# Linear attention with a mixture of depths: one stretch of transposes, products and turns per slot, the first batch's numbers from its own 0/1 rows, and later relus

## The chip, the cores and the metric

The kernel runs on one core of one Trainium2 chip. The metric is the device time of one execution in microseconds (us); lower is better. The core has five engines with a queue of instructions each, which run in order and wait for one another by semaphores: TensorE (PE in the profile, its weight loads PEld), VectorE (DVE), ScalarE (ACT), GpSimd (POOL) and SyncE (SP), which here issues most of the transfers.

## The reference

Inputs are q, k, v (8 batches, 8 heads, 576 rows, 64 columns), a gate vector (512), two expert matrices w1 (512 x 1024) and w2 (1024 x 512), and a capacity of 128. All is f32.

```python
q_s = softmax(q, over the 64 columns)
k_s = softmax(k, over the 576 rows)
kv  = einsum('bhsd,bhse->bhde', k_s, v)
x   = einsum('bhsd,bhde->bhse', q_s, kv)   # heads side by side: x is (8, 576, 512)
scores = x @ w_gate                        # per batch
out = x
for each batch b:
    top = the 128 rows with the highest score
    ye  = relu(x[b, top] @ w1) @ w2
    out[b, top] = x[b, top] + sigmoid(scores[b, top])[:, None] * ye
```

So attention is computed for all rows, and the expert network for 128 of 576 rows of each batch.

## The kernel before

**Units and slots.** The work is cut into 16 units, four heads of one batch each, two to a batch. Slot s of the main program is built around unit s. For a unit the kernel takes the exponential of k (`k_exp`, ScalarE, L238) and copies v beside a column of ones (`v_copy`, L250, one buffer), multiplies k by v on TensorE (`kv_mm`, L262), and makes a weight of the result on VectorE (`kv_out`, L271 to L275). It takes the exponential of q (`q_exp`, L246), transposes it on TensorE (`q_t`, L299), copies it out of PSUM on ScalarE (L304), and multiplies (`x_mm`, L324): that is product x. VectorE takes row sums and scores from it (`x_sums`, L335 and L336, and `score`, L362), scales it (`x_scale`, L342, two halves), and SyncE stores it to the output (`x_store`, L353). Transposes and product x share two PSUM buffers: the next slot's transposes need this slot's scalings done.

**Choosing rows.** When a batch is complete (odd slots), `score_row` spreads its scores over all partitions by five transposes and two ScalarE copies (L379, L382). Five comparisons on VectorE give each row its rank (`compare`, L390), `hits` turns ranks into 0/1 rows (L406), and `find` multiplies them by a table of row numbers and scores (L415) and sums the result (L419 to L421). `fetch` reads the chosen rows back from the output by an indirect transfer from GpSimd's queue (L428, tile `xr`). `gate` and `gated` make the sigmoid (L450; L455, L456). `turn` transposes the fetched rows on TensorE (L463) and copies them on ScalarE (L469, tile `xT`). For the first batch the rows are chosen on the chip instead (`select`, L438 and L442: its own f32 0/1 rows in the buffer of `hT`), and the numbers come later, in slot 4, from a second `hits(0)` and `find(0)`.

**Expert work.** It is cut into pieces that a generator hands out; the due count of pieces rises by n at each `pieces(n)` of a slot. Batches 0 and 1 are computed alone (L488, L497; a piece counts two), the others in pairs by a scheme of seven block products instead of eight, with precombined weights and rows (L573, L624; a piece counts one). A pair has 56 units: seven steps of four pieces for the first matrix, then seven for the second. Units 0 to 63 are the two single batches, 64 to 119 pair 2 and 3, 120 to 175 pair 4 and 5, 176 to 231 pair 6 and 7. After a step come sums on VectorE (`add`, L584; `after_p3`, L584 and L599 to L601; `after_p4`, L604 and L605) or copies and relus on ScalarE (L581, L587). The steps of the second matrix end in output sums (`begin`, L632 and L633; `end`, L637). Two PSUM banks serve a pair, so a step that starts a bank anew must wait for the sum that reads it.

**Order.** `tc.manual_schedule()` holds the program's order on every engine: what is written first is queued first. A slot of 7 and later before the change runs on TensorE: transposes of q for unit s, k by v for unit s + 1, four units, product x, in even slots the find for the batch finished before, then units again, in odd slots a score row and a turn among them. Slots 3 to 6 are a loop of their own. After slot 15 the rest of the pairs follows, with the last batch's find at unit 160 and its turn at 174.

## Time and profile before

| what | us |
|---|---|
| median of three runs | 210.12 |
| lowest and highest | 209.05, 212.19 |
| profiled execution, its own time | 209.2 |
| its span, first to last instruction | 207.5 |
| TensorE busy | 187.3 |
| VectorE busy | 128.7 |
| ScalarE busy | 102.7 |
| GpSimd busy | 69.2 |

The transposes of q of slots 3 to 15 begin at 35.06, 44.01, 53.14, 62.39, 70.81, 82.40, 90.56, 99.20, 110.64, 121.40, 130.88, 141.28 and 151.84 us of the span; the last product ends at 199.4. TensorE's f32 products appear as two passes each, so a unit of the first matrix is four records and one of the second is two. A timeline row gives start, duration, engine, line, operation, output and inputs, shapes and the number of merged instructions; in brackets stands the idle time before it and what ended it. A group's row gives busy microseconds and the mean of one in ns. TensorE's records overlap by some 0.07 us at their ends, so starts are compared with starts.

### The profile page before, as it was taken

What the parts mean: (1) busy time and instruction counts of PE and PEld (TensorE: products, weight loads), DVE (VectorE), ACT (ScalarE), POOL (GpSimd) and SP (SyncE); (2) the same over time, 40 slices, a digit from 0 to 9 for tenths busy, and PEclk for the clock granted to TensorE, in tenths of its full rate; (3) what the DMA queues carried; (4) which work ended last, traced back from release to release, by engine and by line L of the source; (5) the groups of instructions that cost most, each with busy time, mean ns of one, the idle gap of its engine ahead of it and who ended that gap; (6) DMA issues with size and microseconds to landing.
All of it is one profiled execution on the core that took longest, in us unless ns stands there. A gap on an engine that the chain in (4) does not pass through costs nothing.

```text
span 207.5 us, 7034 instructions
## 1 busy us (share of the span) xinstructions
PE 187.3 (90%) x2925; PEld 158.9 (77%) x2927; DVE 128.7 (62%) x422; ACT 102.7 (49%) x168; POOL 69.2 (33%) x122
## 2 busy tenths in 40 slices
PE   6699799999999896999989999999899989999940
PEld 2477699976579883769879888799899879998830
DVE  7236985498189345965993998269949934535010
ACT  2453344866668738946496495728243222322100
POOL 8022200200870742089824133135012264601230
PEclk9889999999999999999999999999999999999995
DMA  5999999999989899958977868959136113110020
GB/s 171 349 374 386 372 369 386 362 346 335 284 282 294 236 336 360 343 158 267 353 268 221 297 173 275 259 165 263 57 86 155 40 51 104 51 52 5 3 101 13
DMA packets 35210, 46.68 MB, mean 225 GB/s; under 512 B 2401, under 2 KB 28001, under 8 KB 35170
## 3 DMA queue, kind: packets, MB, share of 16 engines
q1 hardware_dynamic: 33616, 41.62, 62.2%
q0 software_dynamic: 1280, 4.20, 6.1%
q8 instruction: 25, 0.41, 0.8%
q10 hardware_dynamic: 274, 0.33, 0.5%
q14 instruction: 15, 0.12, 0.2%
HBM read 34.61 MB, written 11.53 MB: 222 GB/s over the span
## 4 chain that ended last, share of the span: by engine, by line
PE 49%; DVE 16%; DMA 12%; ACT 7%; POOL 5%; issue 5%; SPq 1%; POOLq 0%; ACTq 0%; DVEq 0%
PE mm L624 15%; PE mm L573 11%; DMA v<-in_v_dram 8%; PE x L324 7%; DVE junk L390 6%; PE tp L262 4%; PE mm L488 4%; DMA k<-in_k_dram 2%; PE mm L442 2%; PE x L299 2%; DMA q<-in_q_dram 2%; POOL tw L540 2%; ACT ke L238 2%; DVE xs L342 1%; SPq L121 1%
## 5 line engine op out<-in xcount | busy, mean ns | idle before, releaser
L390 DVE SCALAR_TENSOR_TENSOR junk<-srow,s,stairs 128x576 bf16<-128x576 f32 x40 | 35.2, 880 | 5.2 <-ACT srow L382 3.0
L324 PEld LDWEIGHTS x<-kv_w,qT 64*64 64x64 f32 (+1 forms) x1120 | 21.8, 135 | 7.5 <-ACT qT L304 3.8
L304 ACT COPY qT<-x 128x640 f32<-128x640 f32 (+1 forms) x30 | 17.8, 643 | 18.5 <-PE x L299 10.5
L324 PE MATMUL x<-kv_w,qT 64*64 64x66 f32 (+1 forms) x1120 | 24.6, 224 | 1.9 <-ACT qT L304 1.4
L262 PE MATMUL tp<-v_ones,ke 128*64 128x65 f32 x640 | 23.4, 230 | 2.3 <-DVE v_ones L250 1.7
L342 DVE TENSOR_TENSOR xs<-x,qrec 128x640 f32<-128x640 f32 x32 | 24.7, 815 | 0.0
L262 PEld LDWEIGHTS tp<-v_ones,ke 128*64 128x64 f32 x640 | 21.1, 143 | 4.0 <-issue 2.3
L624 PE MATMUL mm<-w,hT 128*128 128x256 f32 x96 | 22.9, 383 | 0.2 <-ACT hT L604 0.2
L428 POOL DMA_INDIRECT xr<-out_dram,idx x8 | 8.1, 1016 | 44.0 <-DVE no L421 16.1
L246 ACT ACTIVATE qe<-q 128x640 f32<-128x640 f32 (+1 forms) x32 | 20.2, 687 | 2.6 <-DMA q<-in_q_dram 2.6
L238 ACT ACTIVATE ke<-k 128x1280 f32<-128x1280 f32 x16 | 20.4, 1276 | 0.9 <-DMA k<-in_k_dram 0.9
L624 PEld LDWEIGHTS mm<-w,hT 128*128 128x128 f32 x96 | 17.6, 190 | 2.8 <-ACT hT L604 0.5
L335 DVE RECIPROCAL qrec<-x 128x10 f32<-128x10 f32 x32 | 7.0, 218 | 19.1 <-PE x L324 18.9
L573 PE MATMUL mm<-xT,w 128*128 128x128 f32 x144 | 18.4, 278 | 0.0
L624 PE MATMUL mm<-tw,hT 128*128 128x256 f32 x72 | 17.4, 382 | 0.7 <-DVE o L637 0.7
L573 PEld LDWEIGHTS mm<-xT,w 128*128 128x128 f32 x144 | 17.1, 192 | 0.5
L250 ACT COPY v_ones<-v 128x1280 f32<-128x1280 f32 x12 | 15.1, 1260 | 4.3 <-DMA v<-in_v_dram 4.3
L488 PE MATMUL mm<-xT,w 128*128 128x128 f32 x128 | 16.8, 282 | 0.0
L497 PE MATMUL mm<-w,hT 128*128 128x512 f32 x32 | 16.2, 614 | 0.0
L488 PEld LDWEIGHTS mm<-xT,w 128*128 128x128 f32 x128 | 15.0, 191 | 0.6
L624 PEld LDWEIGHTS mm<-tw,hT 128*128 128x128 f32 x72 | 13.4, 190 | 2.5 <-DVE o L637 0.8
L364 POOL TENSOR_TENSOR s<-s_all,valid_r 128x5 f32<-128x5 f32 x8 | 1.6, 198 | 40.6 <-DVE s_all L362 40.5
(138 smaller groups left out, 302.0 us busy)
## 6 DMA issues: line engine op xcount, KB each, us to landing
q<-in_q_dram SPq DMA_DIRECT2D x32, 288.0 KB, 6.4
v<-in_v_dram SPq DMA_DIRECT2D x16, 320.0 KB, 5.8
out_dram<-xs SPq DMA_DIRECT2D x16, 320.0 KB, 4.8
k<-in_k_dram SPq DMA_DIRECT2D x15, 320.0 KB
k<-in_k_dram SPq DMA_DIRECT2D x16, 256.0 KB
v<-in_v_dram SPq DMA_DIRECT2D x16, 256.0 KB, 5.3
out_dram<-xs SPq DMA_DIRECT2D x16, 256.0 KB, 5.1
w<-in_moe_w_dram SPq DMA_DIRECT2D x4, 512.0 KB
```

Source lines behind the costliest of these rows:

```text
L238: nc.scalar.activation(out=ke, in_=raw["k"][u % LD], func=AF.Exp)
L246: nc.scalar.activation(out=st["qe", u][:, r0:r1], in_=qr[:, r0:r1], func=AF.Exp)
L250: copy(out=v_ones[:, :, :, :D], in_=raw["v"][u % LD])
L262: nc.tensor.matmul(out=kv[part(h), i], lhsT=ke[:, 2 * h + i, r], rhs=vo[:, 2 * h + i, r], start=(r == 0), stop=(r == N2))
L304: nc.scalar.copy(out=to, in_=src)
L324: nc.tensor.matmul(out=to[:, r * C:(r + 1) * C], lhsT=lhsT, rhs=kw[part(i), a], start=True, stop=True)
L342: nc.vector.tensor_mul(xs[b][:, :, qd, :, a].rearrange("p r i d -> p i r d"), x[:, :, :, :D], rec.to_broadcast([P, 2, R, D]))
L390: nc.vector.scalar_tensor_tensor(junk, st["srow", b], st["s", b][:, r:r + 1], not_before[r], op0=OP.subtract, op1=OP.is_ge, accum_out=st[" ...
L488: nc.tensor.matmul(out=h_ps[:, f % HT * m:(f % HT + 1) * m], lhsT=w1[:, d, f * P:(f + 1) * P], rhs=xT[:, d, :m], start=(d == 0), stop=(d = ...
L497: nc.tensor.matmul(out=st["y", b][:m], lhsT=st["hT", b][:, f // HT, f % HT, :m], rhs=w2[:, f], start=(f == 0), stop=(f == KF - 1))
L573: nc.tensor.matmul(out=out_ps[:, f * m:(f + 1) * m], lhsT=w[:, k, f * P:(f + 1) * P], rhs=x()[:, k], start=first and f == 0 and k == 0, st ...
L624: nc.tensor.matmul(out=ps_of[to][:m, :HD], lhsT=st["hT", a][:, n, f, :m], rhs=w[:, f], start=first and f == 0, stop=f == HT - 1, skip_grou ...
```

## The change

It has three parts.

- **First batch's numbers.** `find_selected(0)` is called right after the products of slot 2. It copies the table of numbers to f32 on GpSimd and multiplies the f32 0/1 rows that `select` made by it; the three small sums (`found`) follow after `kv_out(3)`. The `hits(0)` and `find(0)` of slot 4 go; batch 1 takes their place there, one step earlier. `gate(0)` moves to slot 3, `gated(0)` to slot 4.
- **Relus.** The two relus of a pair that follow a sum (after steps 2 and 5) are issued after the second piece of the next step instead of right after the sum.
- **Slots 7 to 15.** The four units between k by v and product x go. In odd slots the turn stands between k by v and product x; so transposes, k by v, turn and product x are one stretch, with three units ahead of product x in slot 15 alone. The copy of v for slot s + 2 follows product x (in slot 7 it follows the score row and the exponential of k). The two scalings stand apart, with three units between them in odd slots and two in even ones. The other units follow the score row or the find. In slot 6 the exponential of k for slot 8 moves ahead of the gate.

```diff
+    def find_selected(b):
+        wide = md.tile([P, R, NV], F32, tag="wide", name="wide", bufs=1)
+        nc.gpsimd.tensor_copy(out=wide, in_=vals[:, place(b)])
+        hit = st["select"][1]
+        c_ps = bank("tp", 2)
+        for r in range(R):
+            nc.tensor.matmul(out=c_ps[:m, :NV], lhsT=hit[:, r, :m], rhs=wide[:, r], start=(r == 0), stop=(r == N2))
+        return lambda: found(b, c_ps)
...
         def after_p2():
             add("side1", 0)
-            relu(0)
         def after_p7():
             add("chain1", 3)
-            relu(3)
...
+        later = {id(after_p2): lambda: relu(0), id(after_p7): lambda: relu(3)}
...
+                    then = [lag] if lag and f == 1 else []
+                    if f == HT - 1:
+                        then.append(after)
...
     x_mm(2, 1)
+    found_0 = find_selected(0)
...
     kv_out(3)
+    found_0()
...
-            hits(0 if first else here)
-        if s == FIRST + 2:
+            hits(here)
+        if first:
             gated(0)
...
-            find(0 if first else here)
-            if first:
-                hits(here)
-            else:
-                fetch(here)
+            find(here)
+            fetch(here)
...
-            pieces(3)
-            gate(0 if first else here)
-            if first:
-                find(1)
-                fetch(1)
-                gate(1)
+            pieces(2)
+            if s == SETTLED - 1:
+                k_exp(s + 2)
+            pieces(1)
+            gate(here)
             prepared(PREPARE[s])
             if s == SETTLED - 1:
-                k_exp(s + 2)
                 v_copy(s + 2, nc.scalar)
...
         if on:
             kv_mm(s + 1)
             q_exps(s + 1)
+        if odd:
+            turn(ends - 1)
+        if on:
             kv_out(s + 1)
-            if s + 2 < NU:
-                v_copy(s + 2, nc.scalar)
-        if odd:
-            gated(ends - 1)
-        pieces(4 if on else 3)
+        else:
+            pieces(3)
         attend(s)
         if not odd:
             find(here)
             fetch(here)
-        scale(s)
+        if more and s > SETTLED:
+            v_copy(s + 2, nc.scalar)
+        x_scale(s, 0)
+        if odd:
+            gated(ends - 1)
+        pieces(3 if odd else 2)
+        x_scale(s, 1)
+        x_store(s)
         if s + 3 < NU:
             load(s + 3, "q")
...
-        if s + 2 < NU and not odd:
-            k_exp(s + 2)
-        pieces(2 if s < PAIRED or not on else 4)
         if odd:
+            if not on:
+                pieces(1)
             score_row(here)
-            if s + 2 < NU:
+            if more:
                 k_exp(s + 2)
-        left = 4 if s < PAIRED - 1 else 3 if s < PAIRED else 5
-        if odd and on:
-            compares(here, 1)
-            pieces(left // 2)
-            turn(ends - 1)
+                if s == SETTLED:
+                    v_copy(s + 2, nc.scalar)
             if ends > 2:
                 size(ends - 1)
             if ends > 2 and ends % 2 == 0:
                 combine_rows(ends - 2, ends - 1)
-            compares(here, 1)
-            pieces(1)
-            compares(here, 1)
-            pieces(left - left // 2 - 1)
...
+            if on:
+                compares(here, 1)
+                pieces(3 if many else 2)
+                compares(here, 1)
+                pieces(4 if many else 2)
+                compares(here, 1)
+                pieces(3 if many else 2 if s == PAIRED - 1 else 3)
+            else:
+                compares(here, 3)
+                pieces(4)
+                compares(here, 2)
+                hits(here)
+                pieces(2)
+        else:
             pieces(2)
...
+            if more:
+                k_exp(s + 2)
+            pieces(2)
             gate(here)
             prepared(PREPARE.get(s, 0))
-            pieces(left - 1)
+            pieces(7 if many else 4)
```

`many` holds from slot 10 on, `more` while a slot s + 2 exists, `on` while a slot s + 1 exists. A slot hands out 10 units in slots 7 and 8, 9 in slot 9 and 13 in slots 10 to 14, as before; slot 15 hands out 13 instead of 11.

More of the change, by code (lines that the diff above doesn't have):

```diff
@@ L416, in find, with found @@
                              start=(r == 0), stop=(r == N2))
+        found(b, c_ps)
+    def find_selected(b):
[6 more added lines that the diff above has]
+        return lambda: found(b, c_ps)
+    def found(b, c_ps):
         no = sl.tile([P, 2], F32, tag="no", name="no", bufs=4)
@@ L648, in pair, with piece @@
                   ("chain2", 3, tw2[:, 2], False, lambda: end("chain2", b, 0, rows=st["xr", b], last=True))]
+        def piece(product, what, f, then):
+            product(*what, f)
+            for step in then:
+                step()
+        lag = None
         for steps, product in ((steps1, product1), (steps2, product2)):
@@ L651, in pair @@
                 for f in range(HT):
-                    yield 1, lambda what=what, f=f, product=product, after=after: (
-                        product(*what, f), after() if f == HT - 1 else None)
+                    then = [lag] if lag and f == 1 else []
+                    if f == HT - 1:
+                        then.append(after)
+                    yield 1, lambda product=product, what=what, f=f, then=then: piece(product, what, f, then)
+                lag = later.get(id(after))
     def single(b):
@@ L918 @@
         kv_out(s + 1)
+        if s == FIRST:
+            gate(0)
         if odd:
@@ L940 @@
         here = ends if odd else ends - 1
-        on = s + 1 < NU
+        on, more = s + 1 < NU, s + 2 < NU
+        many = s >= PAIRED
         q_t(s, 0)
@@ L982 @@
                 combine_rows(ends - 2, ends - 1)
-            compares(here, 1)
-            pieces(1)
-            compares(here, 1)
-            pieces(left - left // 2 - 1)
-        elif odd:
-            compares(here, 3)
-            pieces(4)
-            compares(here, 2)
-            hits(here)
+            if on:
[12 more added lines that the diff above has]
+        else:
             pieces(2)
-            turn(ends - 1)
-            size(ends - 1)
-        else:
-            pieces(1)
+            if more:
+                k_exp(s + 2)
+            pieces(2)
             gate(here)
             prepared(PREPARE.get(s, 0))
-            pieces(left - 1)
+            pieces(7 if many else 4)
     last = B - 1
```

## The prediction

> **What bounds the kernel now.** I read the page first: busy shares and granted clock.
>
> ```profile
> PE 187.3 (90%) x2925; PEld 158.9 (77%) x2927; DVE 128.7 (62%) x422; ACT 102.7 (49%) x168; POOL 69.2 (33%) x122
> PEclk9889999999999999999999999999999999999995
> ```
>
> TensorE is busy for 90% of the span, and from the fourth slice to the last but one its granted clock is 0.9 or more. So time is won only where TensorE waits or does less. Next I read who TensorE waited for (columns: microseconds in total, times, longest):
>
> ```profile
> PE x L324 <- ACT qT L304: 1.4, 2, 1.2
> PE tp L463 <- ACT srow L382: 1.6, 1, 1.6
> PE tp L415 <- DVE hit L406: 1.1, 2, 0.7
> PE mm L624 <- DVE o L637: 0.7, 1, 0.7
> ```
>
> With a 0.60 in slot 7 (below) these are nearly all of its waits from slot 3 on: 1.1 for the 0/1 rows in slots 4 and 14 (L415), 1.6 for the turn of slot 7, 1.4 for copies of turned q in slot 10, 0.7 for an output sum in the last stage. Some 5.4 us can be won, no more. The cause of the copies' wait is on ScalarE: its relu stands first in its queue and waits for VectorE's sum.
>
> ```profile
> ACT hT L587 <- DVE hT L584: 13.9, 6, 3.9
> ```
>
> Then TensorE in order of time, for slots 9 to 11 and the last stage (columns: start, microseconds, line, shapes, count):
>
> ```profile
> 94.11 0.73 PE L324 MATMUL x<-kv_w,qT 64*64 64x66 f32 x33
> 95.44 1.16 PE L573 MATMUL mm<-xT,w 128*128 128x128 f32 x8
> 96.44 0.71 PE L379 MATMUL tp<-ident,s_all 128*128 128x128 f32 x5
> 96.98 0.61 PE L573 MATMUL mm<-xT,w 128*128 128x128 f32 x4
> 97.72 0.66 PE L463 MATMUL tp<-ident,xr 128*128 128x128 f32 x4
> 98.22 1.06 PE L573 MATMUL mm<-xT,w 128*128 128x128 f32 x8
> 99.20 0.78 PE L299 MATMUL x<-ident,qe 64*128 64x64 f32 x18
> 99.91 1.39 PE L262 MATMUL tp<-v_ones,ke 128*64 128x65 f32 x40
> 101.23 2.05 PE L573 MATMUL mm<-xc,sw 128*128 128x128 f32 x16
> ...
> 106.30 0.28 PE L415 MATMUL tp<-vals,hit 128*128 128x5 bf16 x5
> ...
> 166.91 1.99 PE L624 MATMUL mm<-tw,hT 128*128 128x256 f32 x8 [0.72 <-DVE o L637]
> ...
> 174.36 3.73 PE L573 MATMUL mm<-xT,w 128*128 128x128 f32 x32
> 177.93 3.74 PE L573 MATMUL mm<-xc,sw 128*128 128x128 f32 x32
> ```
>
> From start to start these give the prices that I use: transposes of q 0.70 (99.20 to 99.91), k by v 1.32 (to 101.23), product x 1.33 (94.11 to 95.44), score row 0.54 (96.44 to 96.98), a turn 0.50 (97.72 to 98.22). Eight units of expert work (32 records) take 3.57 (174.36 to 177.93), so one unit is 0.44. From 166.91, where unit 160 begins, TensorE hardly stops to the end, so what the change does to the start of unit 160 it does to the time.
>
> **The change part by part, up to the end of product x in slot 9.** Before, that is 95.44, with 68 units done.
>
> ```profile
> 28.14 2.94 PE L442 MATMUL mm<-hT,xs 128*128 128x128 f32 x24
> ...
> 51.11 0.28 PE L415 MATMUL tp<-vals,hit 128*128 128x5 bf16 x5 [0.46 <-DVE hit L406]
> 51.25 1.96 PE L497 MATMUL mm<-w,hT 128*128 128x512 f32 x4
> ...
> 72.19 1.39 PE L262 MATMUL tp<-v_ones,ke 128*64 128x65 f32 x40 [0.60 <-ACT v_ones L250]
> ```
>
> *First batch's numbers.* Five products in f32 are added after slot 2, each as two passes. No row has a pass with 128 columns of weights and five of data. The nearest in weights is L442, 24 passes in 2.94, 0.12 each, so 1.2 at most; the bf16 form took 0.14 for five (51.11 to 51.25), so 0.3 for ten at least. The weights are those of L442, so I take 1.1. TensorE runs without a wait there: it is on the path. Removed in slot 4 is the second find with its wait, 0.46 + 0.14 = 0.60. The copy of numbers on GpSimd, the three small sums and the missing 0/1 rows on VectorE lie beside TensorE's work there.
>
> *Slot 7.* The copy of v for slot 9 moves behind the score row and the exponential of k, so the turn's wait of 1.60 goes. The turn itself now stands behind k by v, at 72.19 + 1.32 = 73.51, and needs the rows fetched in slot 6:
>
> ```profile
> 68.95 1.00 POOL L428 DMA_INDIRECT xr<-out_dram,idx  x1 [7.71 <-DVE krec L271]
> ```
>
> ```profile
> DMA to landing us min/median/max: 3.4/4.3/5.2
> ```
>
> Landing 3.4 to 5.2 after 68.95 is 72.35 to 74.15: a wait of 0 to 0.65; I take 0.3. Product x, and all behind it on TensorE, is queued behind that turn. The 0.60 before k by v stays, because the exponential and the copy of v that it waits for still come behind the relu.
>
> *Slot 8.* ScalarE, the copy of v done, still has a size and a relu ahead of the copies of turned q:
>
> ```profile
> 78.65 1.26 ACT L250 COPY v_ones<-v 128x1280 f32<-128x1280 f32 x1 [4.29 <-DMA v<-in_v_dram]
> ...
> 83.30 1.16 ACT L304 COPY qT<-x 128x640 f32<-128x640 f32 x2
> ```
>
> The copy can't start before 78.65, when v has landed, whatever TensorE does. With product x drawn forward over four units, the two copies (1.16) are late by something between nothing and their own length; with TensorE some 1.3 ahead there I take 0.3. In exchange TensorE goes from k by v to x without expert work between them, two changes of operand shape fewer: eight passes before the transposes of q took 0.98 (98.22 to 99.20) against 0.89 by the unit's price, so 0.1 a change, -0.2.
>
> *Order.* By the end of product x in slot 9 four units fewer are done (-1.76) and one turn more (+0.5). Sum: 1.1 - 0.6 - 1.6 + 0.3 + 0.3 - 0.2 - 1.8 + 0.5 = -2.0, that is 93.4 with 64 units done.
>
> **From there VectorE decides.** In every even slot the find stands directly behind product x and waits for the 0/1 rows, and they come behind five comparisons. VectorE's prices:
>
> ```profile
> 93.51 0.15 DVE L455 TENSOR_SCALAR g<-g 128x1 f32<-128x1 f32 x1
> ...
> 99.63 0.42 DVE L548 TENSOR_TENSOR xc<-xT 128x256 f32<-128x256 f32 x1
> ...
> 155.53 0.22 DVE L335 RECIPROCAL qrec<-x 128x10 f32<-128x10 f32 x1 [0.16 <-PE x L324]
> ...
> 156.12 1.54 DVE L342 TENSOR_TENSOR xs<-x,qrec 128x640 f32<-128x640 f32 x2
> ...
> 160.32 0.69 DVE L584 TENSOR_TENSOR hT<-mm,hT 128x512 f32<-128x512 f32 x1
> ...
> 162.98 0.81 DVE L390 SCALAR_TENSOR_TENSOR junk<-srow,s,stairs 128x576 bf16<-128x576 f32 x1
> ...
> 165.03 0.82 DVE L406 TENSOR_TENSOR hit<-slot_no,rank 128x640 bf16<-128x640 f32 x1
> 165.78 0.68 DVE L605 TENSOR_TENSOR hT<-hT 128x512 f32<-128x512 f32 x1
> 166.38 0.48 DVE L637 SCALAR_TENSOR_TENSOR o<-mm,g,o 128x256 f32<-128x256 f32 x1
> ```
>
> ```profile
> L390 DVE SCALAR_TENSOR_TENSOR junk<-srow,s,stairs 128x576 bf16<-128x576 f32 x40 | 35.2, 880 | 5.2 <-ACT srow L382 3.0 <-POOL s L365 1.2
> ```
>
> Sums to the first scaling 0.6 (155.53 to 156.12), two scalings 1.54, the gate's pair 0.3, a pair of combined rows 0.85, a comparison 0.88, one sum 0.69, the four of after_p3 2.66 (160.32 to 162.98), hits 0.82, the subtraction of after_p4 0.68, an output sum 0.48.
>
> Slot 9 to find in 10: VectorE 0.6 + 1.54 + 0.3 + 0.85 + 4.4 + 0.69 + 0.82 = 9.2; TensorE eight units 3.5, score row 0.54, q 0.7, k by v 1.32, x 1.33, changes of shape 0.3: 7.7. So it waits 1.5, and the find is at 102.6. Before, four units were done by 106.30; this wait takes the place of the 1.2, which the later relu does remove. Then find, 13 units, q, k by v, turn, x: 0.14 + 5.7 + 0.7 + 1.32 + 0.5 + 1.33 + 0.2 = 9.9: slot 11's x ends at 112.5.
>
> Slot 11 to 12: VectorE 0.6 + 1.54 + 0.3 + 2.66 + 4.4 + 0.68 + 0.82 = 11.0, TensorE 13 units and the rest 9.9: a wait of 1.1, find at 123.5. Unit 104 needs an output sum that is now queued on VectorE behind kv_out, the sums to the first scaling and that scaling: in time, or late by up to about 0.9 with six units (2.6) as cover. I add 0.45. Slot 13's x: 123.5 + 9.9 + 0.45 = 133.9.
>
> Slot 13 to 14: VectorE 0.6 + 1.54 + 0.3 + 0.85 + 3 x 0.48 + 4.4 + 0.82 = 9.95 against 9.9: nothing. Find 143.8. Unit 132 needs the sum of unit 127, which stands behind the second scaling: 0 to 1, I add 0.5. With q, turn and three units in front of x, slot 15's x ends 9.9 + 0.5 later, at 154.2.
>
> Slot 15: VectorE 0.6 + 1.54 + 0.3 + 2.66 + 4.4 + 0.68 + 0.82 + 0.48 = 11.5, TensorE 20 units 8.8 and 0.7: it waits 2, and unit 160 starts at 165.7 against 166.91. I round the gain to 1.0, since hand-overs between engines are left out.
>
> The profiled execution took 209.2 (span 207.5, 1.7 around it), 0.9 under the median of 210.12 and close to the fastest run. The sum is 208.2 on the profile and 209.1 on the median; I take 208.7.
>
> **Moved at no cost.** A slot's store and its load of q go to SyncE's queue some three units later, behind the second scaling; the q that waits there is used two slots on, some 18 us, and would cost only if it came that late. The fetch stands in GpSimd's queue ahead of the weights' sums as before; from slot 8 on its find lies ten or thirteen units, q and k by v ahead of the turn, 6.4 or 7.7, against 5.2 for the longest landing and about 1 for the sums between find and fetch. The copy of v behind product x has the units after it as cover, 1.26 against 4.4 or more; if they were gone, k by v of the next slot would wait for all of it.
>
> **Rivals.** *TensorE stays the bound.* If comparisons come soon enough, none of the new waits appears: 1.6 + 1.4 + 0.7 + 0.7 + 0.6 go, four changes of shape (0.8) too, 1.1 is added: -4.7, 204.5 on the profile. For it: in slot 10 of before the find waited for nothing (the row at 106.30 shows no idle time). Against: five comparisons alone are 4.4 and no part of the change takes work from VectorE after slot 4.
>
> *GpSimd stretches comparisons (slower).* Comparisons differ widely:
>
> ```profile
> L390 DVE SCALAR_TENSOR_TENSOR junk<-srow,s,stairs x40: 799/819/2189, 23.1 to 163.8; 128x576 bf16<-128x576 f32 x40
> ```
>
> ```profile
> L633 POOL TENSOR_TENSOR o<-o,xr x9: 714/725/1314, 122.3 to 194.8; 128x256 f32<-128x256 f32 x9
> ```
>
> The longest is 2189 ns against a median of 819, and a sum on GpSimd took 1314 instead of 725 while comparisons ran at 163. If each stretch between x and find has such meetings (two with the combined rows in slots 9 and 13, one each in 11 and 15), six at 0.72 add 4.3 to stretches that VectorE now sets: 212.5 on the profile. It decides from the second meeting on, which eats the 1.0. Against: my 0.88 is a mean that holds some of them already. [...]
>
> *The change doesn't free ScalarE.* The relu two pieces on may still find its sum undone, since the sum stands behind comparisons; copies then wait as before and the time is 209 to 210.
>
> **How the numbers follow.** Forecast 0.58 (207 to 210), TensorE stays the bound 0.15 (204.5 to 206), stretched comparisons 0.19 (210.5 to 213), ScalarE not freed 0.08. The range reaches to the middle of the first and third: 205.4 to 211.8. About 2% is what a measurement of this kernel can tell from no change, 4.2 us: faster by more than that 0.14, within 0.81, slower by more 0.05.
>
> **What would show it.** Right: TensorE's waits at L463 for the srow copy and at L324 for qT gone; new waits of 1 to 2 us at L415 for hit in slots 10 and 12 and in the last stage; f32 find near 1.1. Wrong: if no wait at L415 exceeds 0.5 in slots 10 to 15, VectorE isn't the bound and the time falls to 205; if TensorE waits at L463 for the DMA by over 1 us in several slots, the fetch is too late, and the time rises.

## The result, and the profile after

The changed kernel takes 211.0 us (median of 20 executions, 208.39 to 212.67) against 209.37 for the kernel before (20 executions, 206.74 to 212.81). The ratio is 1.010 with a 95% interval of 1.0062 to 1.0138: slower by about 1%, where 208.7 was forecast, a gain. Ratios here and below leave out an execution that lies more than 1.5% above its kernel's fastest, so the medians of all executions stand beside them.

The profiled execution after took 210.88 us (span 209.1) against 209.2 (207.5). Line numbers have moved: `fetch` is L441, the turn L476, its copy L482, the pair's products L586 and L636, the sums L597, `end` L649; `find` (L415), `hits` (L406) and `compare` (L390) are where they were. First the page's shares and clock, and TensorE's waits from slot 7 on, beside the 0.60 in slot 7 that stays:

```profile
PE 189.0 (90%) x2930; PEld 160.6 (77%) x2932; DVE 127.5 (61%) x421; ACT 102.8 (49%) x168; POOL 70.2 (34%) x123
PEclk9999999999999999999999999999999969999996
```

```profile
PE tp L415 <- DVE hit L406: 5.0, 3, 2.0
PE tp L476 <- DMA xr<-out_dram,idx: 0.8, 1, 0.8
PE tp L476 <- DVE krec L271: 0.3, 1, 0.3
PE mm L586 <- DVE o L649: 0.2, 1, 0.2
```

The waits for the srow copy (1.6), for qT (1.2 in slot 10) and for the last output sum (0.7) are gone, and so is the second find of slot 4 with its 0.46. In their place stand three waits for 0/1 rows, 5.0 together, and two short ones in front of the turns. One digit of the clock line is new, too: a 6 in the 33rd slice, just behind the last find. TensorE in order of time:

```profile
30.72 1.28 PE L426 MATMUL tp<-wide,hT 128*128 128x5 f32 x10
31.93 1.39 PE L262 MATMUL tp<-v_ones,ke 128*64 128x65 f32 x40
...
73.24 0.63 PE L476 MATMUL tp<-ident,xr 128*128 128x128 f32 x4 [0.33 <-DVE krec L271]
...
91.47 0.63 PE L476 MATMUL tp<-ident,xr 128*128 128x128 f32 x4 [0.84 <-DMA xr<-out_dram,idx]
...
93.35 0.38 PE L586 MATMUL mm<-xT,w 128*128 128x128 f32 x1
...
102.61 0.28 PE L415 MATMUL tp<-vals,hit 128*128 128x5 bf16 x5 [1.52 <-DVE hit L406]
...
124.01 0.28 PE L415 MATMUL tp<-vals,hit 128*128 128x5 bf16 x5 [1.47 <-DVE hit L406]
...
142.99 0.50 PE L262 MATMUL tp<-v_ones,ke 128*64 128x65 f32 x9 [0.17 <-issue]
143.43 1.08 PE L324 MATMUL x<-kv_w,qT 64*64 64x66 f32 x32
...
145.17 0.28 PE L415 MATMUL tp<-vals,hit 128*128 128x5 bf16 x5
...
155.24 0.94 PE L586 MATMUL mm<-xT,sw 128*128 128x128 f32 x6
...
166.86 0.28 PE L415 MATMUL tp<-vals,hit 128*128 128x5 bf16 x5 [2.05 <-DVE hit L406]
167.25 3.11 PE L636 MATMUL mm<-tw,hT 128*128 128x256 f32 x8
170.16 4.23 PE L636 MATMUL mm<-w,hT 128*128 128x256 f32 x16
174.22 1.03 PE L636 MATMUL mm<-tw,hT 128*128 128x256 f32 x4
175.09 0.60 PE L476 MATMUL tp<-ident,xr 128*128 128x128 f32 x4
```

Up to the find in slot 10 this is the forecast to the tenth; the find in slot 12 comes 0.5 later than forecast. The new thing is at 167.25: eight products that took 1.99 before take 3.11, and the turn follows 8.2 us behind the last find. The view of windows shows why; its boundaries are put on a grid of 3.413 us on which all changes of the granted clock in these traces fall; here it falls at 167.98, rises at 171.39 and falls again at 205.52, 34.13 or ten times 3.413 later (columns: window, length, busy time and count of PE, PEld, DVE, ACT, POOL, granted clock, DMA share, GB/s):

```profile
161.15:164.56 3.41, 3.41 (x17) 2.88 (x16) 3.34 (x8) 0.47 (x1) 0.72 (x1) 1.00 0.11 37
164.56:167.98 3.42, 1.26 (x10) 0.87 (x9) 3.05 (x10) 0.68 (x2) 0.90 (x2) 1.00 0.00 0
167.98:171.39 3.41, 3.41 (x9) 2.66 (x9) 0.20 (x2) 0.47 (x1) 1.26 (x2) 0.50 0.28 77
171.39:174.80 3.41, 3.41 (x17) 3.00 (x16) 0.86 (x2) 0.00 (x0) 1.25 (x2) 1.00 0.31 82
```

In the window that holds the wait TensorE is busy for 1.26 of 3.42 us. In the next one it works without a pause, at half the clock, and gets through 9 records instead of 17. That is 1.7 us lost behind a wait of 2.05.

VectorE and GpSimd show why the wait is 2.05 (VectorE's rows and GpSimd's, each in order of time):

```profile
155.96 0.81 DVE L342 TENSOR_TENSOR xs<-x,qrec 128x640 f32<-128x640 f32 x1
...
162.12 1.17 DVE L390 SCALAR_TENSOR_TENSOR junk<-srow,s,stairs 128x576 bf16<-128x576 f32 x1
...
165.54 1.27 DVE L406 TENSOR_TENSOR hit<-slot_no,rank 128x640 bf16<-128x640 f32 x1
```

```profile
161.95 0.72 POOL L645 TENSOR_TENSOR o<-o,xr 128x256 f32<-128x256 f32 x1 [4.13 <-ACT o L644]
165.40 0.72 POOL L645 TENSOR_TENSOR o<-o,xr 128x256 f32<-128x256 f32 x1 [2.72 <-ACT o L644]
```

One comparison (1.17 instead of 0.82) and the 0/1 rows themselves (1.27 instead of 0.82) run beside a sum on GpSimd and take 0.8 longer together. These are meetings of the second rival, 0.35 and 0.45 each where it took 0.72, and they come in the stretch on VectorE that TensorE then waits for.

### The profile page after: what moved, and what is told of

The parts are those of the page before. It is cut to its first block, busy times and chain, and to the rows that moved or that the text cites. A ratio compares the mean times of both kernels' runs of the same rounds, so it can differ in the third digit from the quotient of the medians.

```text
span 209.1 us, 7044 instructions
## 1 busy us (share of the span) xinstructions
PE 189.0 (90%) x2930; PEld 160.6 (77%) x2932; DVE 127.5 (61%) x421; ACT 102.8 (49%) x168; POOL 70.2 (34%) x123
## 4 chain that ended last, share of the span: by engine, by line
PE 65%; DVE 20%; DMA 5%; issue 4%; ACT 1%; POOL 1%; POOLq 0%; DVEq 0%; ACTq 0%
PE mm L586 13%; PE mm L636 13%; PE x L324 10%; PE tp L262 7%; PE mm L501 7%; DVE junk L390 7%; PE mm L510 5%; DVE xs L342 4%; PE x L299 3%; DMA xr<-out_dram,idx 3%; DMA v<-in_v_dram 2%; PE mm L455 2%; PE tp L476 2%; PE x L292 1%; DVE o L649 1%
## 5 line engine op out<-in xcount | busy, mean ns | idle before, releaser
L390 DVE SCALAR_TENSOR_TENSOR junk<-srow,s,stairs 128x576 bf16<-128x576 f32 x40 | 33.7, 843 | 1.1 <-ACT srow L382 0.2
L324 PE MATMUL x<-kv_w,qT 64*64 64x66 f32 (+1 forms) x1120 | 25.2, 224 | 0.6 <-DVE qT L302 0.4
L342 DVE TENSOR_TENSOR xs<-x,qrec 128x640 f32<-128x640 f32 x32 | 25.2, 814 | 0.0
L262 PE MATMUL tp<-v_ones,ke 128*64 128x65 f32 x640 | 22.5, 224 | 1.2 <-ACT v_ones L250 0.6
L636 PE MATMUL mm<-w,hT 128*128 128x256 f32 x96 | 23.0, 389 | 0.0
L262 PEld LDWEIGHTS tp<-v_ones,ke 128*64 128x64 f32 x640 | 20.1, 137 | 3.0 <-issue 1.3
L441 POOL DMA_INDIRECT xr<-out_dram,idx x8 | 8.1, 1016 | 39.9 <-DVE krec L271 18.2
L636 PEld LDWEIGHTS mm<-w,hT 128*128 128x128 f32 x96 | 18.4, 196 | 2.5
L636 PE MATMUL mm<-tw,hT 128*128 128x256 f32 x72 | 18.3, 401 | 0.1
L586 PE MATMUL mm<-xT,w 128*128 128x128 f32 x144 | 17.8, 277 | 0.2 <-DVE o L649 0.2
L586 PEld LDWEIGHTS mm<-xT,w 128*128 128x128 f32 x144 | 16.9, 192 | 0.7 <-DVE o L649 0.6
L636 PEld LDWEIGHTS mm<-tw,hT 128*128 128x128 f32 x72 | 14.0, 198 | 2.5 <-DVE o L649 0.6
L645 POOL TENSOR_TENSOR o<-o,xr 128x256 f32<-128x256 f32 x9 | 6.9, 772 | 26.7 <-ACT o L644 26.1
L510 PE MATMUL mm<-w,hT 128*128 128x512 f32 x32 | 15.3, 605 | 0.0
```

The source lines that it names most:

```text
L262: nc.tensor.matmul(out=kv[part(h), i], lhsT=ke[:, 2 * h + i, r], rhs=vo[:, 2 * h + i, r], start=(r == 0), stop=(r == N2))
L324: nc.tensor.matmul(out=to[:, r * C:(r + 1) * C], lhsT=lhsT, rhs=kw[part(i), a], start=True, stop=True)
L342: nc.vector.tensor_mul(xs[b][:, :, qd, :, a].rearrange("p r i d -> p i r d"), x[:, :, :, :D], rec.to_broadcast([P, 2, R, D]))
L390: nc.vector.scalar_tensor_tensor(junk, st["srow", b], st["s", b][:, r:r + 1], not_before[r], op0=OP.subtract, op1=OP.is_ge, accum_out=st[" ...
L510: nc.tensor.matmul(out=st["y", b][:m], lhsT=st["hT", b][:, f // HT, f % HT, :m], rhs=w2[:, f], start=(f == 0), stop=(f == KF - 1))
L586: nc.tensor.matmul(out=out_ps[:, f * m:(f + 1) * m], lhsT=w[:, k, f * P:(f + 1) * P], rhs=x()[:, k], start=first and f == 0 and k == 0, st ...
```

## The experiments

The theory after the result: the new waits for 0/1 rows take up what slots 7 to 9 win, and the last one, 2.05 long, lets the clock fall for one window, which makes the loss. Rivals: the wait itself, without the clock, is the price; the first part's f32 products are the price; the later relus are.

**e1_busy.** TensorE is kept at work during the last wait, by products whose result nothing reads.

```diff
+    junk_x = ps.tile([P, 2, 512], F32, tag="x", name="x", bufs=2)
+    for _ in range(9):
+        nc.tensor.matmul(out=junk_x[:, 0], lhsT=ones_b[:, :P], rhs=ones_b, start=True, stop=True)
     find(last)
```

> The changed kernel with nine products of ones (bf16, 512 columns, into an unused PSUM tile) put ahead of the last find, where TensorE waited 2.05 us; nothing reads them. Theory (the long wait at the last find makes TensorE's granted clock fall to half for one window of 3.4 us): the nine take some 1.9 us in the place of the wait, unit 160 starts at 167 to 167.6 as in the changed kernel, the granted clock stays 1.00 from 165 to 175 us, and the time falls by 1.7 to about 209.3, a ratio to the kernel before of 1.00. [...]

Measured: 209.77 (207.54 to 211.07), ratio 1.0035 (0.9986 to 1.0084) to a median of 210.05 before. TensorE:

```profile
165.41 2.11 PE L1034 MATMUL x<-ones_b 128*128 128x512 bf16 x9
167.62 0.28 PE L415 MATMUL tp<-vals,hit 128*128 128x5 bf16 x5
...
174.16 0.60 PE L476 MATMUL tp<-ident,xr 128*128 128x128 f32 x4
```

From find to turn it is 6.5 us instead of 8.2, with the same real work and the find no earlier behind its comparisons, and the granted clock is 1.00 from 165 to 173. Useless work in the wait takes the fall of the clock away, and by the medians 1.2 us with it (two measurements on different chips, with intervals that overlap). The clock is part of the price.

**e2_find_late.** Find and fetch of slots 10, 12 and 14 stand behind four units instead of directly behind product x.

```diff
-        if not odd:
+        if not odd and not many:
             find(here)
             fetch(here)
...
             pieces(2)
+            if many:
+                find(here)
+                fetch(here)
```

> The changed kernel with find and fetch of slots 10, 12 and 14 put behind four units instead of directly behind product x. Theory (these finds wait for VectorE's comparisons, 1.5 us each in slots 10 and 12): both waits at L415 go, product x of slot 15 ends some 3 us earlier than in the changed kernel (152.3 against 155.2), and the time falls by 2.5 to 3, to about 208.3, a ratio of 0.995, with the wait at the last find still there. Rival (the fetched rows come too late for the turn in the next slot, now four units nearer): the turns of slots 11 and 13 wait 1 to 2 us each and the time stays near 211, a ratio of 1.01.

Measured: 221.11 (219.82 to 224.42), ratio 1.0596 (1.0523 to 1.0669). The waits at the finds of slots 10 and 12 are gone, but the turns wait for their rows instead, and three windows fall to half clock (behind waits of 3.08, 3.75 and 2.0):

```profile
PE tp L476 <- DMA xr<-out_dram,idx: 9.2, 5, 3.7
PE tp L415 <- DVE hit L406: 2.0, 1, 2.0
```

The edit did two things: it put the fetch late, and behind the slot's store, which touches the same tensor as the fetch reads. In slot 10 the landing took from 105.54 to 111.78, 6.2 us; in slot 14 the fetch wasn't issued until the store just ahead of it had ended. So it shows what a late fetch costs (more than the rival expected), and not what a late find would.

**e3_before_wait.** The kernel before, with the last batch's last comparison done four times (the same numbers each time), so that its last find waits.

```diff
             compares(here, 2)
+            for _ in range(3):
+                compare(here, R - 1)
             hits(here)
```

> The kernel before with the last comparison of the last batch done four times instead of once (the same numbers are written), so that the 0/1 rows come 2.6 us later. Theory (a wait of over 2 us at the last find makes the clock fall): TensorE waits 2.5 us there, the granted clock falls to half for 3.4 us right behind it, and the time grows by 2.6 + 1.7 = 4.3, a ratio of 1.02. Rival (no fall by a wait of this length): it grows by 2.6, a ratio of 1.0125, and the clock stays 1.00.

Measured: 213.73 (211.68 to 215.54), ratio 1.0221 (1.0154 to 1.0288).

```profile
170.12 0.29 PE L415 MATMUL tp<-vals,hit 128*128 128x5 bf16 x5 [2.91 <-DVE hit L406]
```

```profile
171.00:173.00 2.00, 1.88 (x5) 1.52 (x6) 0.67 (x6) 0.20 (x1) 1.01 (x1) 0.50 0.00 0
173.00:175.00 2.00, 2.00 (x6) 1.64 (x5) 0.00 (x0) 0.06 (x1) 0.00 (x0) 0.50 0.44 131
```

A wait of 2.91 is put into a kernel that had none there, and the clock is halved from 170.15 to 176.98, two windows. The loss, 3.7 us by the medians, is more than the wait.

**e4_tail.** The changed kernel, with eight more units between the third and the fourth comparison of the last batch, so that its find stands behind unit 168 instead of 160, and the turn six units later.

```diff
-                pieces(4)
+                pieces(12)
                 compares(here, 2)
                 hits(here)
-                pieces(2)
...
-    upto(last_pair - 16)
+    upto(last_pair - 8)
     find(last)
...
-    upto(last_pair - 12)
+    upto(last_pair - 4)
...
-    upto(last_pair - 2)
+    upto(last_pair + 4)
     turn(last)
```

> The changed kernel with the last stage in another order: twelve units instead of four between the third and the fourth comparison of the last batch, its find at unit 168 instead of 160 and its turn at 180 instead of 174. Theory (the wait at the last find and the clock that falls behind it cost 2.0 + 1.7): no wait over 0.3 at the last find, granted clock 1.00 to the end, time lower by 3 to 3.7, about 207.5, a ratio of 0.99. Rival (the time is moved to the last turn, whose rows come late, or to VectorE's later sums): TensorE waits over 1.5 us at the last turn or behind it and the time stays at 210 to 211, a ratio of 1.005 to 1.01.

Measured: 207.94 (207.06 to 210.85), ratio 0.9957 (0.991 to 1.0004) to 210.05. The find at 167.61 waits for nothing, the clock is full from 5.5 to 200.09, and TensorE's last product starts at 197.69 instead of 201.06. Product x of slot 15 ended 0.48 earlier by itself, so 2.9 us are won by moving the last find: 2.05 of wait and 1.7 of clock, less a new wait of 0.79 for a sum at 178.27.

**e5_find_three and e6_both.** e5: find and fetch of slots 10, 12 and 14 behind three units, but ahead of the scalings and the store. e6: e5 and e4 together.

```diff
         attend(s)
         if not odd:
+            pieces(3 if many else 0)
             find(here)
             fetch(here)
...
-            pieces(7 if many else 4)
+            pieces(4)
```

> The changed kernel with find and fetch of slots 10, 12 and 14 behind three units, but still ahead of both scalings, the store and the load of that slot, so that the fetch leaves no later than in the changed kernel. Theory (the finds wait for the 0/1 rows, and the run with four units lost by its late fetch, not by the order of TensorE): the waits at L415 in slots 10 and 12 fall from 1.5 to 0.2 at most, the fetch is issued at most 0.5 after its place in the changed kernel, the turns wait less than 1, product x of slot 15 ends 2 to 2.6 earlier (152.5 to 153.1 against 155.1 on a run with the same start), and the time falls by about 2.3 to 208.7 with the last wait and its fallen clock still there, a ratio of 0.998. Rival (VectorE is the bound itself, so that TensorE's order changes nothing): the waits move to the last find or to the sums, and the time stays at 211, a ratio of 1.01.

> The find behind three units in slots 10, 12 and 14 together with the reordered last stage (twelve units ahead of the last two comparisons, last find at unit 168, last turn at 180). Theory: both gains add, -2.3 and -3, no wait over 1 us at any find, granted clock 1.00 to the last product, about 205.7, a ratio of 0.983 and below both kernels. Rival (one cures what the other cures, since both only move the same VectorE work): no better than the reordered last stage alone, 207.9, a ratio of 0.996.

Measured: e5 208.0 (205.0 to 209.28), ratio 0.9865 (0.9788 to 0.9942); e6 204.85 (203.73 to 206.77), ratio 0.9824 (0.9765 to 0.9883), both to 209.19. In e5 the finds of slots 10 to 14 wait 0.10 at most, product x of slot 15 ends at 152.42 instead of 155.24, and the last find still waits:

```profile
PE tp L415 <- DVE hit L406: 2.1, 1, 2.1
```

In e6 that one is gone too, and the page's clock line has no gap from the fifth slice to the last but one:

```profile
PE 186.4 (92%) x2932; PEld 158.9 (79%) x2932; DVE 128.4 (64%) x421; ACT 102.2 (51%) x168; POOL 70.4 (35%) x123
PEclk9999999999999999999999999999999999999995
```

VectorE is busy for 128.4 us, against 127.5 in the changed kernel. What changed is only how many units TensorE has between a comparison and its find. e6 is faster than both kernels.

**e7_first_alone.** The kernel before with the first part of the change only (`find_selected`, and slots 3 to 6, the exponential of k that moves in slot 6 with them).

```diff
     x_mm(2, 1)
+    found_0 = find_selected(0)
...
-            hits(0 if first else here)
+            hits(here)
...
-            find(0 if first else here)
+            find(here)
```

> The kernel before with the first part alone: the first batch's numbers from its own 0/1 rows behind the products of slot 2, and no second find in slot 4. Theory (five f32 products cost about 1.25 on TensorE's path, the find and the wait that go give 0.85 back): the transposes of slot 5 begin 0.3 to 0.5 later against the start of the run, the time is 0.4 higher, a ratio of 1.002. Rival (VectorE relieved of 0.82 and of one wait frees more than that): 0.5 to 1 lower, a ratio of 0.997.

Measured: 210.35 (207.55 to 211.65), ratio 1.0026 (0.9985 to 1.0068) to 209.19. The ratio is as expected; by the medians of all executions it is 1.2 us more. In its profile the turn of slot 7 waited longer than in the kernel before:

```profile
80.83 0.66 PE L476 MATMUL tp<-ident,xr 128*128 128x128 f32 x4 [2.39 <-ACT srow L382]
```

The wait ends at 80.83, as it does before (80.95) and in e3 (80.74), though the first transposes of q began at 16.12 here, at 17.40 before and at 16.31 in e3. That wait had an end of its own, and TensorE's earlier or later start went into it. In e3 and here, where it was 2.4 to 2.5, a window at half clock followed (81.40 to 84.82 and 82.14 to 85.55).

**e8_relu_at_once.** The changed kernel with the relus right behind their sums again.

```diff
             add("side1", 0)
+            relu(0)
...
             add("chain1", 3)
+            relu(3)
...
-        later = {id(after_p2): lambda: relu(0), id(after_p7): lambda: relu(3)}
+        later = {}
```

> The changed kernel with both relus issued right after their sums, as before the change. Theory (ScalarE's relu holds back the copies of turned q in slot 10, but the find would wait for VectorE anyway): product x of slot 10 waits about 1.2 at L324, the find's wait in slot 10 shrinks from 1.5 to 0.5 or less, and the time grows by 0.5 at most, to 211 to 211.5, a ratio of 1.01 to 1.0125. Rival (the later relus are what the change wins by): it grows by 1.2 or more, to over 212.2, a ratio of 1.016 or more.

Measured: 209.82 (one of its 14 executions took 467.1, the others 208.02 to 213.51), ratio 1.0038 (0.9993 to 1.0083): not slower than the changed kernel, so a miss. Its slot 10 shows both halves: x waits 1.26 for qT again, at 102.39, and the find behind it, at 104.20, doesn't wait. Where the find waits for VectorE, freeing ScalarE ahead of it shortens one wait and lengthens the next. In this profile the wait for qT and the shorter ones around it left the window 0.59 busy, and a window at half clock followed (104.55 to 107.96).

**e10_both_relu.** The same edit on e6, where no find waits.

> The version with both repairs (find behind three units in slots 10, 12 and 14, eight more units ahead of the last find), with the two relus issued right after their sums again, as before the change. Theory (the later relu frees ScalarE for the copies of turned q, which shows only where the find no longer sets the pace): product x of slot 10 waits about 1.2 to 1.4 for qT, nothing behind it hides that, and the ratio is 0.988 to 0.992 against 0.982 with the later relus. Rival (the relus' move is worth nothing here either, as in the changed kernel): 0.979 to 0.986.

Measured: 208.03 (205.94 to 210.92), ratio 0.9929 (0.9878 to 0.998) to 209.73, a little above the theory's 0.988 to 0.992, and far from the rival's.

```profile
101.07 0.33 PE L324 MATMUL x<-kv_w,qT 64*64 64x66 f32 x2 [1.46 <-ACT qT L304]
```

The wait for qT, 1.46, now reaches the end: x of slot 15 ends 3.6 us later than in e6. Of this 0.9 was there at the end of slot 9, ahead of the relus, and the rest beyond 1.46 isn't explained. By the ratios the later relus are worth about 1%, once the find gives way.

**e9_slots_alone and e12_slots_again.** The changed kernel without the first part, twice (the exponential of k in slot 6 goes back with it), and **e11_after_again**, the changed kernel on the chip of the second.

```diff
-    found_0 = find_selected(0)
...
-    found_0()
...
-            find(here)
-            fetch(here)
+            find(0 if first else here)
+            if first:
+                hits(here)
+            else:
+                fetch(here)
```

> The changed kernel with the first part undone: the first batch's numbers come again from the second 0/1 rows in slot 4, with the wait there; relus and slots 7 to 15 as changed. Theory (the loss comes from the three waits for 0/1 rows and from the half-clock window behind the last of them; the first part costs its 1.2 in f32 products and gives back 0.85): the waits of about 1.5, 1.5 and 2.05 at the find stay, the clock falls to half behind the last, and the ratio to before is 1.004 to 1.010. Rival (the f32 products of the first part are what makes the change slower): without them it isn't slower, 0.994 to 1.001.

> The changed kernel itself, as the measure for the next kernel on one chip. Theory A (the first part costs no more than its own products, 0.45 net): the ratio to before is again 1.006 to 1.014, and 0.002 to 0.004 above that of the kernel without the first part. Theory B (the first part makes the whole loss): 1.006 to 1.014, and 0.007 or more above the kernel without it. Theory C (the loss was measured too high, and all of these differ by less than the measurement tells): 1.001 to 1.006.

> The changed kernel with the first part undone, a second time, on the chip of the changed kernel. Theory A: 1.003 to 1.010, under the changed kernel by 0.002 to 0.004. Theory B: 0.996 to 1.002, under it by 0.007 or more. Theory C: 0.999 to 1.004, within 0.003 of it.

Measured: e9 209.85 (208.12 to 213.77), ratio 1.0002 (0.9955 to 1.0048) to 209.73; e11 210.8 (209.05 to 212.6), 1.0121 (1.0021 to 1.0222), and e12 208.95 (206.74 to 211.69), 0.9963 (0.9911 to 1.0014), both to 209.97. By their ratios both measurements of e9's kernel lie with the rival: without the first part the kernel is not slower than before. The three waits are there nonetheless, and e9's trace holds a pair that explains the clock:

```profile
98.56:101.97 3.41, 1.46 (x82) 1.32 (x75) 3.31 (x8) 2.33 (x4) 1.58 (x2) 1.00 0.92 256
101.97:105.38 3.41, 3.41 (x17) 3.41 (x18) 2.87 (x14) 0.00 (x0) 1.73 (x2) 0.50 0.82 282
163.41:166.82 3.41, 2.02 (x10) 1.44 (x8) 3.34 (x8) 0.47 (x1) 0.72 (x1) 1.00 0.00 0
166.82:170.24 3.42, 2.64 (x16) 2.30 (x17) 1.68 (x7) 0.53 (x2) 1.01 (x1) 1.00 0.06 8
```

The wait of 1.95 in slot 10 lies in one window of the grid, which leaves 1.46 of work in it, and the next window is at half. The last wait, 2.05, lies across two windows with 2.02 and 2.64 of work, and the clock stays. The profiled e12 tells of the start: its transposes of q began at 17.46, and x of slot 9 ended at 94.62 because the turn ahead of it waited for its rows:

```profile
92.74 0.63 PE L476 MATMUL tp<-ident,xr 128*128 128x128 f32 x4 [1.62 <-DMA xr<-out_dram,idx]
```

**e13_first_bf16, e15_both_bf16, e14_both_slots, e16_both_again.** What the first part costs: e13 is the changed kernel and e15 is e6, each with the five products in bf16; e14 is e6 without the first part; e16 is e6 a second time.

```diff
-        wide = md.tile([P, R, NV], F32, tag="wide", name="wide", bufs=1)
-        nc.gpsimd.tensor_copy(out=wide, in_=vals[:, place(b)])
-        hit = st["select"][1]
+        hit = md.tile([P, R, P], BF16, tag="hit", name="hit", bufs=1)
+        nc.scalar.copy(out=hit[:, :, :m], in_=st["select"][1][:, :R, :m])
...
-            nc.tensor.matmul(out=c_ps[:m, :NV], lhsT=hit[:, r, :m], rhs=wide[:, r], start=(r == 0), stop=(r == N2))
+            nc.tensor.matmul(out=c_ps[:m, :NV], lhsT=hit[:, r, :m], rhs=vals[:, place(b), r],
```

> The changed kernel with the first part in bf16: ScalarE copies the 0/1 rows to bf16 and the five products take the table of numbers as it is. If the f32 products, 1.21 of TensorE's time in slot 2, reach the end, they shrink to about 0.3 and the ratio falls by 0.004 (0.9 us) from the changed kernel's 1.010 to 1.012, to 1.005 to 1.008. If the first part costs by what it moves (fetch and gate of batches 0 and 1, slot 6), not by its products, the ratio stays at 1.009 to 1.014. If it costs nothing beside the spread of the runs, 0.999 to 1.005.

> The version with both repairs, with the first part undone. If the first part makes the loss (1.2 to 1.8 us of a run), this beats the version with both repairs by 0.005 or more: 0.972 to 0.979. If the first part costs its 0.4 net alone, within 0.003 of it: 0.979 to 0.986.

> The version with both repairs, and the first part in bf16. TensorE sets the pace in most of that version, so if the f32 products reach the end, this is 0.9 us faster: a ratio of 0.975 to 0.981 against 0.980 to 0.985. If later waits take them up, no difference.

> The version with both repairs a second time, as the measure for the other two on one chip: 0.979 to 0.986, no half-clock window between the start and the last product.

Measured, to 209.26: e13 211.06 (207.0 to 213.9), ratio 0.997 (0.9904 to 1.0036), which rests on two of its six executions; e14 204.63 (203.53 to 206.62), 0.9776 (0.9743 to 0.9808); e15 204.25 (203.97 to 205.09), 0.9779 (0.9751 to 0.9807); e16 205.05 (204.33 to 206.05), 0.9813 (0.9781 to 0.9844). Against e16, e15 is 0.8 faster by the medians and e14 0.4. That is what it should be if in the version without waits the f32 products reach the end and the first part costs 0.4 net; but the intervals overlap, and a cost of 1 us isn't excluded. e13 by itself is unclear: its median says no gain, its ratio says one, and in its trace 0.56 of what bf16 saves went into a wait for ScalarE's copy. But its profiled execution is e11's in slot 15 to within 0.1 us, without the fall of the clock, and so measures that fall. e11, then e13:

```profile
164.75 0.28 PE L415 MATMUL tp<-vals,hit 128*128 128x5 bf16 x5 [2.05 <-DVE hit L406]
165.14 2.85 PE L636 MATMUL mm<-tw,hT 128*128 128x256 f32 x8
...
172.97 0.60 PE L476 MATMUL tp<-ident,xr 128*128 128x128 f32 x4
```

```profile
164.68 0.28 PE L415 MATMUL tp<-vals,hit 128*128 128x5 bf16 x5 [2.05 <-DVE hit L406]
165.07 1.99 PE L636 MATMUL mm<-tw,hT 128*128 128x256 f32 x8
...
171.22 0.60 PE L476 MATMUL tp<-ident,xr 128*128 128x128 f32 x4
```

The same wait of 2.05, ended within 0.07 us; from find to turn 8.22 in the one and 6.54 in the other. In e13 the wait lies across two windows (busy 1.95 of 3.41 and 2.71 of 3.42), in e11 in one (1.26). The fall costs 1.7.

## Why the prediction was wrong

**Its mechanism came as forecast.** The bound moves from TensorE to VectorE behind slot 9, and the finds wait for 0/1 rows:

| step | forecast | profile after |
|---|---|---|
| product x of slot 9 ends | 93.4 | 93.35 |
| find in slot 10, its wait | 102.6, 1.5 | 102.61, 1.52 |
| find in slot 12, its wait | 123.5, 1.1 | 124.01, 1.47 |
| find in slot 14, its wait | 143.8, 0 | 145.17, 0 |
| product x of slot 15 ends | 154.2 | 155.24 |
| last wait, unit 160 | 2, 165.7 | 2.05, 167.25 |

**The step that failed** is this one: "From 166.91, where unit 160 begins, TensorE hardly stops to the end, so what the change does to the start of unit 160 it does to the time." A wait of 2 us was forecast right ahead of unit 160 and counted as 2 us. It cost 2.05 and then, in the profiled execution, 1.7 more: from unit 160 to the last product it took 32.1 before (166.91 to 199.03), 32.1 in e13, where the clock held, and 33.8 after (167.25 to 201.06). e1 and e11 against e13 show that this is the clock and not the work. The waits that the change removed had been 1.6 and shorter in the profile of before; it put a longer one in their place, and the prediction exchanged them at par.

Every change of the granted clock in these traces lies on a grid of 3.413 us, whose phase differs from one execution to the next. In before the clock falls at 8.33, rises at 11.74 and falls again at 202.89: 3.41 us and then 191.15, which is 56 times 3.413. In after the times are 167.98, 171.39 and 205.52: 3.41 and ten times 3.413. Counted from the start of the span the first line of the grid lies at 1.5 in the one and at 0.7 in the other. A window here is one field of that grid. The wait of 2.05 was enough for a fall where it lay in one window (1.26 of 3.42 busy), and not where it lay across two (e13).

**How often the clock falls.** A profile shows one execution, but the mean granted clock was measured in all of them. One window at half clock takes 0.008 from it (1.7 of some 208 us). Behind the last product the clock is at half in all 18 profiles (from 202.89 in before, from 205.52 in after), so the profiles without another such window have means of 0.987 to 0.991, those with one 0.981 to 0.984, the one with two 0.975, those with three 0.966 to 0.970. All executions counted by bounds between these (none from 0.986 up, one from 0.978, two from 0.971):

| kernel | executions | none | one | two | three or more | windows in the mean |
|---|---|---|---|---|---|---|
| before, beside the experiments, without one of 311.5 us | 96 | 37 | 49 | 8 | 2 | 0.74 |
| changed (after, e11) | 26 | 4 | 14 | 7 | 1 | 1.19 |
| changed, without the first part (e9, e12) | 24 | 6 | 13 | 4 | 1 | 1.00 |
| changed, last wait filled (e1) | 12 | 7 | 2 | 3 | 0 | 0.67 |
| changed, last find later (e4) | 12 | 9 | 3 | 0 | 0 | 0.25 |
| both repairs (e6, e16) | 12 | 7 | 5 | 0 | 0 | 0.42 |

From none to one and from one to two the median time of the executions rises by 1.8 and 1.9 us in before and by 1.3 each in the changed kernel. The kernel before pays such windows too, which the prediction left out as well: one at the start in its profile, one behind the turn of slot 7 in e3 and e7. The changed kernel pays 0.45 more per execution. At 1.7 each that is an estimated 0.8 us, about half of the 1.6 by which it is slower; filling the last wait (e1) or moving its find (e4) brings the count to 0.67 and 0.25.

**Terms that were mis-sized.** The last stretch on VectorE was put at 11.5 and took 12.0 (155.24 to 167.25): two meetings with GpSimd's sums, 0.8, which a mean price of a comparison doesn't show for `hits`. The prediction had the rows in its second rival, and priced six such meetings at 0.72. No run shows that price for each: in before the comparison at 163.84 took 1.16 beside one sum on GpSimd, 0.35 longer than 0.81, and the one at 141.80 took 2.19 beside the two instructions of a pair of combined rows, 0.69 longer for each of them; after, the two meetings cost 0.35 and 0.45. Two at 0.4 may have been enough: without them the last wait would have been 1.25, and the window that holds it some 0.6 busy, at which the clock mostly stayed (an estimate from these rows and the count of windows below; no run shows it). Slot 14 cost 0.85 more than forecast; TensorE pauses at 142.82 and runs product x more slowly, for which no cause is visible. From find to find it took 21.2 there and about 21.1 in e1, e4 and e9, but 20.3, the forecast, in e8, e11, e12 and e13.

**Slot 9: right on the average, and hit by luck.** The forecast took 2.0 off a profile whose transposes of q began at 17.40, and the profile after began at 16.02, so the hit at 93.35 proves little by itself. In the ten profiles that have slots 7 to 9 as changed and the f32 products (after, e1, e2, e4, e5, e6, e8, e10, e11, e16), product x of slot 9 ends between 92.09 and 94.72, at 93.4 on the average, with starts from 15.88 to 17.96. Without the first part it ends at 91.99, 94.62 and 95.26 (e9, e12, e14), where the forecast's terms give 92.9. An earlier start gained nothing in the old order: the wait in slot 7 ended near 80.8 in three kernels, and x of slot 9 ended at 95.44 before, but at 96.73 in e3 and 96.78 in e7, which began earlier and fell to half clock behind that wait. Without that wait the turns of slots 7 and 9 stand closer behind their fetches and wait for rows instead: 0.33 and 0.84 after, 0.82 and nothing in e1, 1.62 in slot 9 of e12. The forecast gave the first of these 0.3 and the second nothing, since 6.4 us of cover stood against a longest landing of 5.2. In the profile after, the fetch for the turn of slot 9 was issued 1.9 behind its find, where about 1 was taken, and landed some 5.5 later.

**First batch's numbers.** The f32 products took 1.21 from start to start (30.72 to 31.93) against 1.1 taken; slot 4 gave back the 0.6 of the second find and some 0.2 more. Net 0.4 was expected, and 0.4 it is in these rows and by the medians of e14 and e16.

**Relus.** The wait for qT went, as forecast, and it brought nothing that could be measured, since the find behind it waits for VectorE (e8); where nothing waits behind it, it is worth about 1% (e10).

**What stays open.** Half of the loss is not explained by the number of half-clock windows: among executions with the same number, the changed kernel's were still the longer ones by the medians, 209.6 against 208.1 with none and 210.9 against 210.0 with one, though on different chips (on the one chip where both were counted, that of e11, it is 209.7 against 210.3 with one, in three and eight executions). With the first part the kernel lost about 1% in both measurements, without it nothing in two, a difference of 1.2 to 1.8 us by the medians, where the rows show 0.4 for the part itself. A different share of half-clock windows, 1.19 against 1.00, would add an estimated 0.3. The exponential of k in slot 6 goes back together with the first part in e9, e12 and e14, and no run takes the two apart. That the slots' new order and the relus bring at most a little in this kernel, though they win in e6, is shown; where the remaining 0.5 to 1 us of the first part comes from is not.

## What to carry to other kernels

Before a wait is moved or exchanged, ask how long the new one is and not only what the sum of waits becomes: a wait of 2.05 on TensorE cost 3.75 in the profile after and 2.05 in e13, while those of 1.52 and 1.47 cost no more than their length. The old waits may have such a price too, in executions that the profile didn't show. When the engine that delivers has become the bound, put units of the waiting engine between delivery and use; here three units ahead of each find and eight ahead of the last turned a loss of 1% into a gain of 1.8% with the same work. Before a removed wait is booked as a gain, see whether it ended at a fixed time, because then it was also what took up the jitter ahead of it.

## What the runs showed of the hardware

- **The granted clock went with TensorE's busy share of a window, not with the length of a wait.** Counted over TensorE's records on the grid of 3.413 us, between the first units and the last product: the 12 windows with 0.10 to 0.43 of it busy were each followed by one at half clock, and of the windows with 0.53 to 0.59 one of sixteen. The one is in e8 (2.00 of 3.41 busy), behind a wait of 1.26 with shorter ones around it. In e3 the clock stayed at half for a second window, with 0.79 busy in the first. A wait of 2.05 lowered the clock in e11, where it left 1.26 of one window busy, and not in e13, where it left 1.95 and 2.71 of two; the waits of 1.52 and 1.47 in after did not, and those of 2.91 (e3), 3.08 and 3.75 (e2) did.
- **The clock also fell near the start.** In five of the 18 profiles one window between 8.3 and 13.2 us was at half clock, and the first transposes of q then began at 17.4 to 18.0 instead of 15.9 to 16.4. The window rows of before and after show it, clock in the third column from the end:

```profile
0.00:10.00 10.00, 6.23 (x44) 3.15 (x46) 5.14 (x28) 3.69 (x5) 4.32 (x16) 0.92 0.77 255
10.00:20.00 10.00, 9.04 (x171) 7.53 (x171) 5.17 (x20) 5.26 (x7) 2.50 (x2) 0.91 1.06 380
```

```profile
0.00:10.00 10.00, 7.44 (x57) 3.32 (x58) 5.27 (x29) 3.71 (x5) 4.32 (x16) 1.00 0.76 246
10.00:20.00 10.00, 8.67 (x189) 7.07 (x191) 5.74 (x24) 5.28 (x7) 2.37 (x2) 1.00 1.07 380
```

- **One fetch behind a store of the same tensor** landed 6.2 us after its issue in e2, where the changed kernel's fetch in that slot, issued ahead of the store, took 3.8. Whether the tensor or the store's traffic made it late is not shown.
